# The joint input projection in token blocks of 128 columns instead of 256

## The chip, the cores and the metric

The kernel runs on one core of a Trainium2 chip. The metric is the device time of one execution in microseconds (us). The kernel before takes 576.53 us, the median of three runs from 575.89 to 577.66 us.

## What is computed

Two blocks follow each other. The first is an attention without softmax: a state per head decays with `w` and takes up `k` and `v` at each of 768 steps, for 4 batches of 8 heads of 48 elements. Its output becomes 3072 tokens of 384 elements, and these go through a feed-forward block with a gate.

```python
for t in range(S):
    cur = einsum('bhd,bhe->bhde', u[None] * k[:, :, t], v[:, :, t])
    y[:, :, t] = einsum('bhd,bhde->bhe', r[:, :, t], state + cur)
    state = w[:, :, t][..., None] * state + einsum('bhd,bhe->bhde', k[:, :, t], v[:, :, t])
x = y.transpose(0, 2, 1, 3).reshape(3072, 384)
h = x @ w_in                      # 384 x 2048
g = h * erf(softplus(h))
out = g @ w_out                   # 2048 x 384
```

All of it is fp32.

## The kernel before

The tokens go through in 12 units of 256 tokens (two batches of 128 tokens each, `UNIT = NJ * C` = 2 x 128). For each unit the attention makes `xT`, the unit's tokens with their 384 features on the partitions in three parts (`KT` = 3). The input projection makes the hidden values `h`, 2048 = 16 x 128 features by 256 tokens; softplus and erf on ScalarE and a multiply on VectorE make the gate; the output projection (`project_fast`, line 1245) uses a Strassen-like scheme with 192 columns per matmul. The engines' instructions are issued in an order written out by hand: strings such as `"J u v J J v J z z J"` name the next piece of work of each kind.

For most units the input projection is `hidden` (line 1123): three matmuls of 128 x 128 weights by 256 tokens accumulate one block of 128 features. For the last two units it is `hidden_of_two`. It treats the two units together as a product of 2 x 2 blocks and uses seven products with 128 x 128 weights, or sums of such weights, and tokens, or sums of tokens, instead of eight, and adds the products with the third part of the features. `join_weights` and `join_tokens` make the sums in advance. A `J` in the order is one step of it. Each step calls `add_up` once, which issues matmuls to one of three places in PSUM: `m0` (the tile `y`), `low` and `high` (two banks `pp`). Each place holds 2 x 256 values per partition, the two halves (`e`) in different PSUM banks. Behind `add_up` a copy on ScalarE (lines 1342, 1349, 1355) or a copy or add on VectorE (lines 1345, 1352, 1358, 1359, 1365) takes the sums out. `m0` gathers three products one after the other and is read out after each; the next pair of feature blocks starts it afresh. There are four pairs with seven steps each, and 88 matmuls in all.

The stage starts when the tokens of the last unit are there. While it runs, ScalarE and VectorE also make the gate of what is finished (`u`, `v`, `z` in the order, lines 1382, 1386 and 1390). Behind it come the output projections of the last units.

Two other places serve as measures below: line 641 (`level_products`) and line 748 (`state_part`) are small products of the attention, in which four tiles of TensorE's array are used in turn, each with weights of 32 to 64 columns; line 1033 transposes `k` with eight 128 x 128 matmuls against an identity.

Of the kernel before, what the change touches and what calls it, by code (L numbers as in the profile page):

```python
# [23 lines left out]
NJ = 2  # L24
# [38 lines left out]
def kernel(  # L63
# [14 lines left out]
    nc = tc.nc  # L78
    PSUM = bass.MemoryType.PSUM

    n_steps, _, _, JP, C = rkw.shape
# [52 lines left out]
    def products(shape, n=None):  # L134

        if n is None:
            n = turns["next"]
            turns["next"] = 1 - n
        names = "abc"[: len(shape) - 1]
        return banks[n][:].rearrange(  # L140
            f"p ({' '.join(names)}) -> p {' '.join(names)}", **dict(zip(names, shape[1:]))
        )
# [1138 lines left out]
    def third(g, kk):  # L1281

        return w_in_sb[:, g * FG : (g + 1) * FG, kk * P : (kk + 1) * P]
# [29 lines left out]
    def hidden_of_two():  # L1313

        one, two = n_steps - 2, n_steps - 1
        h11, h21 = (hid.tile([P, FG, UNIT], FP32, name="h")[:] for _ in range(NG))
        h12 = room[:, 2:4].rearrange("p i n -> p (i n)").rearrange("p (f t) -> p f t", t=UNIT)
        h22 = ins.tile([P, 2, JP, C], FP32, name="in")
        h22 = h22[:].rearrange("p x n t -> p (x n t)").rearrange("p (f t) -> p f t", t=UNIT)
        gated[one].extend((h11, h21))  # L1320
        gated[two].extend((h12, h22))
        m0 = y[:, :, 0].rearrange("p e j t -> p e (j t)")
        low, high = (products([P, NE, 2, UNIT], n)[:, :, 0] for n in range(2))

        s1, s2, s3, s4 = turns["joint weights"]
        x, z, t1, t2, t3, t4, less = turns["joint tokens"]
        a11, a12, up, _, a22, down = (third(g, kk) for g in range(NG) for kk in range(KT))

        def add_up(to, start, *factors):

            for k, (a, b) in enumerate(factors):
                for e in range(NE):
                    nc.tensor.matmul(  # L1333
                        to[:, e], lhsT=a[:, 2 * i + e], rhs=b,
                        start=start and not k, stop=True, skip_group_check=True,
                    )

        pairs = FG // 2
        for i in range(pairs):
            f = slice(2 * i, 2 * i + 2)  # L1340
            add_up(m0, True, (a11, x[0]))
            nc.scalar.copy(h11[:, f], m0)
            yield
            add_up(low, True, (a12, x[1]), (up, x[2]))
            nc.vector.tensor_add(h11[:, f], h11[:, f], low)
            chunks.append(h11[:, f])
            yield
            add_up(high, True, (s1, t1))
            nc.scalar.copy(h22[:, f], high)
            yield  # L1350
            add_up(m0, False, (s2, t2))
            nc.vector.tensor_copy(h12[:, f], m0)
            yield
            add_up(low, True, (a22, t4), (down, less))
            nc.scalar.copy(h21[:, f], low)
            yield
            add_up(m0, False, (s3, t3), (down, z[2]))
            nc.vector.tensor_add(h21[:, f], h21[:, f], m0)
            nc.vector.tensor_add(h22[:, f], h22[:, f], m0)
            chunks.append(h21[:, f])  # L1360
            if i < pairs - 2:
                chunks.append(h22[:, f])
            yield
            add_up(high, False, (s4, z[1]), (up, z[2]))
            nc.vector.tensor_add(h12[:, f], h12[:, f], high)
            if i < pairs - 2:
                chunks.append(h12[:, f])
            elif i == pairs - 1:
                chunks.extend(h[:, 2 * i - 2 : 2 * i + 2] for h in (h12, h22))
            yield  # L1370
# [136 lines left out]
    for kk in range(KT):  # L1507
        n = D // KT
        to, of = (x.rearrange("p (e m) -> p e m", e=NE) for x in (apart[:, kk], ident[:]))
# [190 lines left out]
```

## Time and profile before

| | |
|---|---|
| median of three runs | 576.53 us (575.89 to 577.66) |
| profiled execution, first to last instruction (the span) | 575.4 us |
| TensorE matmuls (PE) | busy 568.1 us, 99% of the span, 7336 instructions |
| TensorE weight loads (PEld) | busy 503.9 us, 88%, 7336 instructions |
| VectorE (DVE) | busy 442.7 us, 77% |
| ScalarE (ACT) | busy 358.0 us, 62% |
| GpSimd (POOL) | busy 244.7 us, 43% |
| granted TensorE clock | 1.000 over the whole span |

The profiled execution's own time is known as its span only: the page and the answer on cores both give 575.4 us from the first to the last instruction, 1.1 us below the median of the runs. The last matmul ends at 572.3 us and the last add on VectorE at 572.7 us; behind them comes only the last output's way out.

PE and PEld are two rows of one engine: weights for a following matmul are loaded while the present one runs. Recorded matmuls overlap, so the step from start to start is the time that one costs. Each fp32 matmul of the program appears as two passes in the trace, each a load and a matmul.

### The profile page before, as it was taken

To read this page: it belongs to the slowest core of one execution; us is meant where nothing else is said; L and a number is where in the kernel's file an instruction comes from. 1 tells how busy PE (TensorE), PEld (TensorE's weight loads), DVE (VectorE), ACT (ScalarE), POOL (GpSimd) and SP (SyncE) were. 2 spreads that over 40 slices of the span, in tenths; PEclk is the share of its full clock that TensorE was granted. 3 is DMA by queue.
4 is the path that set the end of the run, shared out by engine and by line. 5 is a ranking of instruction groups with operands and counts; after the bars stand their busy time and mean duration, and the time that the engine had idled before them with its cause. 6 is when DMAs were issued, how large, how long until landed. Compare 5 with 4: busy or idle time off the path is not lost.

```text
span 575.4 us, 16716 instructions
## 1 busy us (share of the span) xinstructions
PE 568.1 (99%) x7336; PEld 503.9 (88%) x7336; DVE 442.7 (77%) x475; ACT 358.0 (62%) x488; POOL 244.7 (43%) x265
## 2 busy tenths in 40 slices
PE   8999999999999999999999999999999999999997
PEld 6688777678998998998998998998898899988997
DVE  7785887999899998798699699599599527255640
ACT  3668777645458858748747756766766661388700
POOL 4567381632885883393384284185173000000000
PEclk9999999999999999999999999999999999999999
DMA  7595662350435325155145145234232201000000
GB/s 263 192 348 214 240 205 68 161 164 3 147 84 168 109 66 171 21 176 166 18 159 167 32 145 172 40 121 162 39 120 74 48 8 37 1 1 2 27 28 27
DMA packets 54081, 63.24 MB, mean 110 GB/s; under 512 B 35160, under 2 KB 40568, under 8 KB 52984
## 3 DMA queue, kind: packets, MB, share of 16 engines
q1 hardware_dynamic: 53624, 61.98, 34.0%
q8 instruction: 57, 0.93, 0.7%
q10 hardware_dynamic: 384, 0.20, 0.1%
q14 instruction: 16, 0.13, 0.1%
HBM read 52.39 MB, written 8.69 MB: 106 GB/s over the span
## 4 chain that ended last, share of the span: by engine, by line
PE 93%; DVE 4%; ACT 2%; issue 1%; POOL 0%; DVEq 0%; ACTq 0%; POOLq 0%
PE m L1245 34%; PE m L1123 33%; PE pp L641 5%; PE pp L1333 4%; PE m L1155 4%; PE y L1333 2%; PE y L673 2%; PE y L699 2%; PE pp L748 2%; PE m L951 1%; DVE in L334 1%; PE pp L960 1%; PE pp L1033 1%; DVE h L1088 1%; ACT rest L267 0%
## 5 line engine op out<-in xcount | busy, mean ns | idle before, releaser
L1123 PE MATMUL m<-xT,w_in_sb 128*128 128x256 f32 x960 | 215.0, 382 | 0.9 <-ACT h L1132 0.7
L1123 PEld LDWEIGHTS m<-xT,w_in_sb 128*128 128x128 f32 x960 | 179.8, 190 | 26.5 <-ACT h L1132 1.4
L334 DVE TENSOR_TENSOR in<-in,tot_sb 128x1024 f32<-128x1024 f32 (+1 forms) x55 | 80.1, 1457 | 12.7 <-PE pp L641 11.4
L1132 ACT COPY h<-m 128x512 f32<-128x512 f32 x80 | 46.1, 580 | 48.5 <-PE m L1123 48.4
L1245 PE MATMUL m<-mixed,h 128*128 128x192 f32 x320 | 56.7, 331 | 0.0
L1245 PE MATMUL m<-w_out_sb,h 128*128 128x192 f32 x320 | 56.2, 329 | 0.0
L1245 PEld LDWEIGHTS m<-mixed,h 128*128 128x128 f32 x320 | 51.8, 190 | 1.0
L1245 PE MATMUL m<-w_out_sb,room 128*128 128x192 f32 x304 | 52.5, 326 | 0.0
L1245 PEld LDWEIGHTS m<-w_out_sb,h 128*128 128x128 f32 x320 | 52.0, 190 | 0.5
L1245 PEld LDWEIGHTS m<-w_out_sb,room 128*128 128x128 f32 x304 | 49.9, 190 | 0.0
L1083 ACT ACT_TABLE_LOAD x30 | 38.5, 1283 | 10.7 <-DVE h L1088 8.5
L463 POOL TENSOR_TENSOR words<-words,own 128x384 f32<-128x384 f32 x21 | 30.1, 1432 | 22.8 <-DVE words L494 13.0
L504 POOL TENSOR_TENSOR words<-words 128x384 f32<-128x384 f32 x28 | 39.7, 1447 | 0.0
L1079 ACT ACT_TABLE_LOAD x30 | 38.5, 1283 | 1.8 <-issue 1.3
L641 PEld LDWEIGHTS pp<-in 48*48 48x48 f32 (+4 forms) x2368 | 30.1, 120 | 10.8 <-issue 3.5
L456 POOL TENSOR_TENSOR own<-rest 128x384 f32<-128x384 f32 x7 | 9.7, 1379 | 61.0 <-ACT o L1251 61.0
L641 PE MATMUL pp<-in 48*48 48x32 f32 (+4 forms) x2368 | 33.9, 206 | 0.2 <-DVE in L334 0.2
L504 POOL TENSOR_TENSOR rk<-words 128x384 f32<-128x384 f32 x28 | 33.4, 1220 | 0.0
L529 DVE TENSOR_REDUCE sums<-rk 128x16 f32<-128x768 f32 (+2 forms) x31 | 31.6, 1020 | 0.0
L408 POOL TENSOR_TENSOR tot_sb<-tot_sb 128x256 f32<-128x256 f32 (+4 forms) x50 | 28.8, 576 | 3.8
L1079 ACT ACTIVATE room<-h 128x1024 f32<-128x1024 f32 x28 | 29.6, 1057 | 0.3
L1245 PE MATMUL m<-mixed,room 128*128 128x192 f32 x160 | 27.7, 327 | 0.0
(206 smaller groups left out, 981.6 us busy)
## 6 DMA issues: line engine op xcount, KB each, us to landing
in<-in_rkw SPq DMA_DIRECT2D x8, 1024.0 KB, 5.2
words<-in_moe_w_in SPq DMA_DIRECT2D x16, 384.0 KB, 5.4
words<-in_moe_w_out SPq DMA_DIRECT2D x16, 384.0 KB, 5.2
words<-in_rk_rows SPq DMA_DIRECT2D x8, 768.0 KB, 6.1
w<-in_rkw SPq DMA_DIRECT2D x11, 512.0 KB
v<-in_v SPq DMA_DIRECT2D x12, 384.0 KB, 5.6
out<-o SPq DMA_DIRECT2D x23, 192.0 KB, 3.0
in<-in_rkw SPq DMA_DIRECT2D x7, 512.0 KB, 5.6
```

The lines of the kernel that those rows point to most:

```text
L334: nc.vector.tensor_mul(halves, halves, view(tots[level - 1], 0, [[1, n], [2, nb], [0, half]]))
L408: nc.gpsimd.tensor_mul(new, pair[:, :, 0], pair[:, :, 1])
L463: engine.tensor_mul(to, to, of[:, :, None, :].to_broadcast([P, NEAR // 2 // half, half, D]))
L504: engine.tensor_mul(to[:, i], r[:, half:], k[:, part * rows + i, None].to_broadcast([P, half, D]),)
L529: nc.vector.tensor_reduce(out=to, in_=of, axis=mybir.AxisListType.X, op=ALU.add)
L641: nc.tensor.matmul(to, lhsT=rk(1, n)[rows(e), s0 : s0 + m], rhs=right, start=True, stop=True,)
L1079: nc.scalar.activation(sp_room, chunks[0], AF.Softplus)
L1083: nc.scalar.activation(at, sp_room, AF.Erf)
L1123: nc.tensor.matmul(ps[:, ff, :], lhsT=w_in_sb[:, g * FG + f + ff, kk * P : (kk + 1) * P], rhs=xT[:, kk, :], start=kk == 0, stop=kk == KT - 1,)
L1132: nc.scalar.copy(h[:, f : f + FT, :], ps[:])
L1245: nc.tensor.matmul(to, lhsT=a[:, f], rhs=b[:, f], start=start and f == 0, stop=f == FG - 1, skip_group_check=True,)
L1333: nc.tensor.matmul(to[:, e], lhsT=a[:, 2 * i + e], rhs=b, start=start and not k, stop=True, skip_group_check=True,)
```

## The change

`add_up` issues, for each of its factors and halves, two matmuls of 128 token columns each instead of one of 256. Both use the same weights `a[:, 2 * i + e]`, and each brings its own load of them. The flag that starts a fresh sum in PSUM (`start`) is set on the first block of columns alone. Nothing else differs: the order of the work, the tiles, the instructions of the other engines and the engines that wait for each other are the same.

```diff
             for k, (a, b) in enumerate(factors):
                 for e in range(NE):
-                    nc.tensor.matmul(
-                        to[:, e], lhsT=a[:, 2 * i + e], rhs=b,
-                        start=start and not k, stop=True, skip_group_check=True,
-                    )
+                    for j in range(NJ):
+                        t = slice(j * C, (j + 1) * C)
+                        nc.tensor.matmul(
+                            to[:, e, t], lhsT=a[:, 2 * i + e], rhs=b[:, t],
+                            start=start and not (k or j), stop=True, skip_group_check=True,
+                        )
```

## The prediction

> **What bounds the kernel now.** I read the page first, for the engine that the end follows; then the windows of the stage that the change touches; then its groups and the chain of waits, for the time of one matmul instruction. From the page:
>
> ```profile
> PE 568.1 (99%) x7336; PEld 503.9 (88%) x7336; DVE 442.7 (77%) x475; ACT 358.0 (62%) x488; POOL 244.7 (43%) x265
> PE 93%; DVE 4%; ACT 2%; issue 1%; POOL 0%; DVEq 0%; ACTq 0%; POOLq 0%
> ```
>
> TensorE is busy 99% of the span and makes up 93% of the chain that ended last; its loader (PEld) is busy less. The stage of the change runs from the first L1333 matmul to the first L1245 matmul behind it (engines in the order PE, PEld, DVE, ACT, POOL, then granted clock, DMA share and GB/s):
>
> ```profile
> 492.57:530.56 37.99, 37.99 (x178) 33.23 (x177) 18.89 (x30) 27.92 (x42) 0.00 (x0) 1.00 0.00 1
> ```
>
> PE has no idle time in these 37.99 us, the clock is granted in full, DVE and ACT are busy 50% and 73%, and no DMA runs to speak of. So what the stage gains or loses on TensorE goes to the end one for one: behind it comes nothing but L1245 work, also back to back.
>
> ```profile
> L1333 PEld LDWEIGHTS pp<-xT,w_in_sb x48: 190/190/190, 493.2 to 530.1; 128*128 128x128 f32 x48
> L1333 PE MATMUL pp<-xT,w_in_sb x48: 379/379/380, 493.4 to 530.3; 128*128 128x256 f32 x48
> ...
> 493.60 2.59 PE pp L1333 x12
> ...
> 530.72 39.00 PE m L1245 x240
> ```
>
> The first two lines are of line 1333's own groups (ns min/median/max), the others of the chain of waits (start, us, what). The recorded 379 ns overlap: twelve passes take 2.59 us, 215.8 ns from start to start. The 192-column passes of L1245 take 39.00 / 240 = 162.5 ns, the 384-column ones of L1155 322.5 ns by their single starts. All three are N x 0.833 + 2.5 ns. The program has 88 matmuls in this stage and the trace 176 passes, so each fp32 matmul is two passes, each with a load of its own. 176 x 215.83 ns = 37.99 us, the stage.
>
> **What is removed, added, moved.** The same columns are moved, 176 x 256 = 352 x 128, in 352 passes, and 352 loads of 128 columns replace 176. No other engine's instruction changes. In the instruction order, waits stay on the first matmul of each product, ahead of the same work.
>
> The price is 352 x (new step) - 37.99 us. Two loops can set the step.
>
> The moving: by the law above a 128-column pass takes 106.7 + 2.5 = 109.2 ns. The trace has such passes, the transposes of L1033 (start, us, what):
>
> ```profile
> 50.44 1.09 PE L1033 MATMUL pp<-ident,in 128*128 128x128 f32 x8
> ```
>
> Taking off the last pass's own 0.272 us and the extra 0.057 us that the first one waits for its weights leaves 0.76 us for seven steps, 109 ns. 352 x 109.17 = 38.43 us: +0.44 us. This is the lower end, because no row has 128 columns moved in less; a gain is excluded, as the columns are the same and only the fixed 2.5 ns per pass doubles. The transposes don't show that the load keeps up: theirs is recorded with 141 ns, the stage's with 190 ns.
>
> The loading: now 216 ns lie between loads, and a load may take most of that unseen. At 128 columns the load (some 107 ns, below) is as long as the pass it must hide under. Rows in which the load sets the step are the level products of L641 and the state products of L748: four small tiles of the array work side by side there, and a tile loads as many columns as it moves, or more. Merged loads of L641 (start, us, what):
>
> ```profile
> 57.30 1.03 PEld L641 LDWEIGHTS pp<-rk 48*64 48x64 f32 x64
> 66.78 0.97 PEld L641 LDWEIGHTS pp<-in 48*60 48x60 f32 x64 [0.33 <-DVE y L276]
> 74.60 0.81 PEld L641 LDWEIGHTS pp<-in 48*48 48x48 f32 x64 [0.33 <-DVE in L334]
> ```
>
> 64 loads are 16 rounds of the four tiles. Without the last load (0.135, 0.132, 0.122 us) and the 0.020 us between the four, 15 rounds take 0.875, 0.818 and 0.668 us: about 58, 55 and 45 ns per round. The single starts give 58.3 ns for 64 loaded columns, 56.7 for 62, 55.0 for 60, 51.7 for 56, 45.0 for 48: exactly N x 0.833 + 5.0 ns, whether 32 or as many columns are moved. So a load overlaps the pass before it on the same tile, but a round of loads has 5 ns of its own where a pass has 2.5. The 64/64 row is this change in small: it takes 58.3 ns where the pass alone would allow 55.8 (as the 64-column passes of L673, with 48 loaded, do).
>
> For 128 columns this law gives 106.7 + 5.0 = 111.7 ns: 352 x 111.67 = 39.31 us, +1.32 us.
>
> The upper end is from the recorded lengths. In all those rounds the step is the load's recorded length less 77 ns (58.3 against 135, 45.0 against 122); 190 - 77 = 113 ns: 39.78 us, +1.79 us. The other way, where TensorE comes to whole-array products without a load in advance (the first L1123 pass behind L748), the next load starts 108 ns after the first one, and the second pass 320 ns after the first, which is 107 ns of load and 213 of moving: this points back to 109. I take 111.7, the value of the rows where load and pass are equally long and both repeat; both ends are kept for the range.
>
> What lies around: the consumers (ACT and DVE copies and adds of 512 columns) wait for a product's last pass, which now starts later but has half the columns (a recorded 272 instead of 379 ns), so they are released at the old time within 10 ns. The tightest turn is bank m0: the add of L1359 ends at 501.90 us and the next pair's first pass starts at 502.07, 0.17 us later. DVE starts its two adds when the last pass ends, and 8 (now 16) passes of `high` hide them: 9 x 215.8 - 379 = 1563 ns before, 17 x 111.7 - 272 = 1627 ns after, so the cover grows by 0.06 us; if it were gone, one add (0.69 us) in each of the three later pairs would cost 2.1 us. The 352 additional instructions on PE and on PEld cost nothing in fetching: elsewhere TensorE takes 352 pairs at 28.7 ns each (from 9 us on), and here one would come each 112 ns.
>
> Sum: 575.4 us span + 1.3 = 576.7 us. The median of the runs, 576.53 us, lies 1.1 us over the span; with the same distance the forecast is 576.53 + 1.32 = 577.85 us, say 577.9.
>
> **Rivals.**
>
> *Moving alone sets the step*, because the 5 ns of the load rounds belong to four tiles taking turns and not to one whole-array load. For: the 108 ns between the first two loads. Against: tile 0's own loop in L748 is 43 ns from load to pass and 2 ns from pass to the next load, with no time in which it visibly waits for the other tiles. 109.2 ns: 576.53 + 0.44 = 577.0 us.
>
> *A load has to be over, by its record, before its pass may start*; this is the one on the other side. The place is each of the 352 passes, the step 190 + 2 = 192 ns: 67.6 us, +29.6, 606.1 us. It decides as soon as less than 192 ns lie between passes. Against: L1245 has 190 ns loads at a step of 162.5 ns, so its passes start 28 ns before the recorded end of their load. What this can't exclude is some of it: a whole-array load that keeps up at a 162 ns step and not at 112. Each 5 ns over the forecast's step costs 1.76 us, so a step of 115 ns is +2.5 us, 579.0 us, and one of 125 ns +6.0 us.
>
> *Load and move in turn.* If the array didn't load while it moves, a step would be 107 + 109 = 216 ns: 352 x 216 = 76.0 us, +38, 614.6 us. Against: L1245 would then need 107 + 162 = 269 ns and shows 162.5. The Trainium skill's page "TensorE: Matmul & The Clock Gate" (Part 3, "The mechanism") has a rule that asks for this: weight loads overlap running matmuls only where the row group differs, and here every load and pass takes all rows. By that rule the trace disagrees, in L1245 (162.5 ns) as in L1333 (215.8 ns).
>
> *The change doesn't do what it says* (the second load of the same weights dropped) is out: the compiled order has four and eight matmuls of 128 columns for each two and four of 256, and a step can't go below the 109.2 ns of the moving in any case.
>
> **How the numbers follow.** Load rounds as in the small rows (111 to 113 ns): 0.65. Moving alone: 0.20. A whole-array load that falls somewhat short (113 to 190 ns): 0.10. A load over by its record: 0.03. In turn: 0.02. About 0.3% (1.7 us) is what a measurement of this kernel can tell from no change: the three runs before lie between 575.89 and 577.66. The forecast of +1.32 us is just inside that bound, and its upper end of +1.79 just outside, so I give a third of the first case (0.22) and nothing else of it to slower, with all of the last three (0.15): 0.37. Faster comes from scatter alone, 0.04, and 0.59 is left for the same. The range goes from the moving alone less the scatter of the runs below their median (577.0 - 0.6, rounded down: 576.3) to the upper end of the load with the scatter above it (576.5 + 1.8 + 1.1 = 579.4), and on to 580.5, which takes in a step of up to 116 ns (+2.8 us) with the same scatter.
>
> **What would show it.** Right: the stage lengthens from 38.0 to about 39.3 us, twelve old passes' work (24 new ones) take 2.68 us in the chain instead of 2.59, PEld is busy through the stage with no gap, recorded matmuls have 272 ns, and everything behind is shifted by the same 1.3 us. If passes start 109.2 ns apart, the first rival holds; above 115 ns a limit has appeared that no row shows here. An idle gap of PE ahead of `y` passes would mean that the m0 turn lost its cover. The prediction is wrong in kind if the stage keeps its length and the span changes elsewhere.

## The result and the profile after

The changed kernel takes 577.75 us, the median of 20 runs (576.81 to 580.40); the kernel before takes 576.64 us, the median of 20 runs beside it (575.50 to 577.96). The ratio is 1.0024, with a 95% interval from 1.0013 to 1.0034: +1.4 us, 0.7 to 2.0. It is not the quotient of the two medians, which lie 1.1 us apart.

The stage of the change in the trace after, from the first matmul of line 1335 to the first of L1245 behind it (columns as before):

```profile
491.34:530.64 39.30, 39.30 (x353) 39.30 (x353) 18.97 (x30) 28.19 (x42) 0.00 (x0) 1.00 0.01 2
```

The stage is 39.30 us long instead of 37.99. DVE and ACT have the work they had; PEld, busy 33.23 us before, is now busy in all of it. The groups of line 1335 (ns min/median/max) and the chain of waits (start, us, what):

```profile
L1335 PEld LDWEIGHTS pp<-xT,w_in_sb x96: 192/192/192, 492.1 to 530.4; 128*128 128x128 f32 x96
L1335 PE MATMUL pp<-xT,w_in_sb x96: 275/275/275, 492.2 to 530.5; 128*128 128x128 f32 x96
```

```profile
492.39 2.68 PE pp L1335 x24
...
530.80 39.00 PE m L1245 x240
```

24 passes take 2.68 us, 111.7 ns each; by their single starts every step in the stage is 111 or 112 ns but the first (110). The output projections behind it take 39.00 us as before.

The span of this execution is 575.5 us, only 0.1 us more than before. That isn't the change: TensorE reached the stage at 491.34 us instead of 492.57. Its first attention product began at 6.48 us instead of 7.09, and its first L1245 pass at 143.52 instead of 144.63, so 1.1 of the 1.2 us were gained in the first quarter, in code that is the same in both. In the experiments below that share this code, the stage begins between 491.79 and 492.93 us: the way to it varies by about as much as the change costs. The stage's own length and the medians of many runs carry the reading.

### The profile page after: what moved, and what is told of

Same layout as the page of the kernel before. It is cut to its first block, busy times and chain, and to the rows that moved or that the text cites. A ratio compares the mean times of both kernels' runs of the same rounds, so it can differ in the third digit from the quotient of the medians.

```text
span 575.5 us, 17068 instructions
## 1 busy us (share of the span) xinstructions
PE 568.4 (99%) x7512; PEld 509.7 (89%) x7512; DVE 439.7 (76%) x475; ACT 358.1 (62%) x488; POOL 245.9 (43%) x265
## 4 chain that ended last, share of the span: by engine, by line
PE 84%; DVE 7%; issue 3%; POOL 2%; DMA 2%; ACT 1%; SPq 0%; DVEq 0%; POOLq 0%; ACTq 0%
PE m L1245 34%; PE m L1123 29%; PE pp L641 5%; PE pp L1335 4%; PE y L1335 2%; DVE in L334 2%; PE y L673 2%; PE m L1155 2%; PE y L699 2%; PE pp L748 1%; DMA words<-in_moe_w_in 1%; PE pp L960 1%; DMA u_sb<-in_u 1%; DVE own L651 1%; POOL w_out_sb L1186 1%
## 5 line engine op out<-in xcount | busy, mean ns | idle before, releaser
L334 DVE TENSOR_TENSOR in<-in,tot_sb 128x1024 f32<-128x1024 f32 (+1 forms) x55 | 78.7, 1431 | 12.1 <-PE pp L641 10.8
L1245 PE MATMUL m<-mixed,h 128*128 128x192 f32 x320 | 56.7, 331 | 0.0
L1245 PE MATMUL m<-w_out_sb,h 128*128 128x192 f32 x320 | 56.1, 329 | 0.0
L1245 PEld LDWEIGHTS m<-mixed,h 128*128 128x128 f32 x320 | 51.7, 190 | 0.9
L1245 PE MATMUL m<-w_out_sb,room 128*128 128x192 f32 x304 | 52.5, 326 | 0.0
L1245 PEld LDWEIGHTS m<-w_out_sb,h 128*128 128x128 f32 x320 | 52.0, 190 | 0.5
L1245 PEld LDWEIGHTS m<-w_out_sb,room 128*128 128x128 f32 x304 | 49.9, 190 | 0.0
L1245 PE MATMUL m<-mixed,room 128*128 128x192 f32 x160 | 27.7, 327 | 0.0
```

What stands on the lines that cost most here:

```text
L334: nc.vector.tensor_mul(halves, halves, view(tots[level - 1], 0, [[1, n], [2, nb], [0, half]]))
L1245: nc.tensor.matmul(to, lhsT=a[:, f], rhs=b[:, f], start=start and f == 0, stop=f == FG - 1, skip_group_check=True,)
```

## The experiments

All times before are medians of the runs of the kernel before on the same chip. The ratios, with their 95% intervals, are again not quotients of the medians; +41.4 and +10.7 us below are differences of medians. The question was which loop sets the 111.7 ns, and whether it would do so elsewhere.

**More passes, the same loads.** Blocks of 64 token columns:

```diff
-                    for j in range(NJ):
-                        t = slice(j * C, (j + 1) * C)
+                    for j in range(4):
+                        t = slice(j * 64, (j + 1) * 64)
```

> Token blocks of 64 columns: 704 passes in the stage. Theory (the load of 128 weight columns sets the step, 128 x 0.833 + 5.0 = 111.7 ns, whatever is moved): the step stays 111.7 ns, the stage takes 704 x 111.67 = 78.6 us, +40.6 us on before, about 617 us in all. Rival 1 (every pass in a dense stream costs its columns and 5 ns): 704 x 58.33 = 41.1 us, +3.1 us. Rival 2 (the moving alone, 2.5 ns per pass): 704 x 55.83 = 39.3 us, +1.3 us.

617.83 us against 576.47, ratio 1.0702 (1.0677 to 1.0727), +41.4 us. The stage, its groups and the chain:

```profile
492.59:571.15 78.56, 78.56 (x706) 78.56 (x705) 19.33 (x30) 31.23 (x44) 0.00 (x0) 1.00 0.01 1
```

```profile
L1335 PEld LDWEIGHTS pp<-xT,w_in_sb x192: 192/192/192, 494.3 to 571.0; 128*128 128x128 f32 x192
L1335 PE MATMUL pp<-xT,w_in_sb x192: 275/275/275, 494.3 to 571.0; 128*128 128x64 f32 x192
```

```profile
494.49 5.36 PE pp L1335 x48
```

78.56 us for 704 passes, 111.6 ns each, with half the columns in each. A pass of 64 columns is recorded with the same 275 ns as one of 128, and only the stage's first pass, whose weights were loaded in advance, with 219. The 56 ns between them are what the step exceeds the moving of 64 columns by (111.7 - 55.8), so I read them as the wait for the load, recorded inside the pass. Both rivals, 58.3 and 55.8 ns per step, are out.

**As many passes, unequal.** Blocks of 192 and 64:

```diff
-                        t = slice(j * C, (j + 1) * C)
+                        t = slice(j * 192, 192 + j * 64)
```

> Blocks of 192 and 64 columns instead of 128 and 128: as many passes, loads and columns. Theory (a step is the longer of the pass and of the load under it): 162.5 ns from a 192-column pass to the next, 111.7 ns from a 64-column pass, 176 x 274.2 = 48.3 us, +10.3 us on before, about 587 us. Rival 1 (5 ns for each pass): 176 x (165.0 + 58.3) = 39.3 us, +1.3 us, no different from 128 and 128. Rival 2 (moving alone): 38.4 us, +0.4 us.

587.16 us against 576.47, ratio 1.0183 (1.0152 to 1.0214), +10.7 us. The stage and the groups of one tile by shape (busy us, mean ns, idle before):

```profile
492.20:540.40 48.20, 48.20 (x354) 48.20 (x353) 19.52 (x30) 29.66 (x43) 0.00 (x0) 1.00 0.01 1
```

```profile
L1335 PE MATMUL pp<-xT,w_in_sb 128*128 128x192 f32 x48 | 13.1, 354 | 0.0
L1335 PE MATMUL pp<-xT,w_in_sb 128*128 128x64 f32 x48 | 7.9, 247 | 0.0
```

The same number of loads, passes and columns as in the change costs 8.9 us more in the stage (48.20 against 39.30), because a long pass can't hide the load that belongs under a short one. The means are those of two kinds of pass. In the single rows half of the 192-column passes last 326 ns and half 382, half of the 64-column ones 219 and half 275: the longer half are those that begin behind a 64-column pass and wait 56 ns for their weights. As the wait is recorded inside the pass, single starts don't show the steps of 162.5 and 111.7 ns that were expected but about 162.5, 55.8, 111.7 and 218 ns in turn; the four add up to the same 548 ns. The 48.20 us rule out a fixed price per pass.

**The load a little shorter.** The load takes 120 or 126 of the 128 weight columns, the pass still 128 tokens:

```diff
-                            to[:, e, t], lhsT=a[:, 2 * i + e], rhs=b[:, t],
+                            to[:120, e, t], lhsT=a[:, 2 * i + e, :120], rhs=b[:, t],
```

> Blocks of 128 tokens, but each load takes 120 of the 128 weight columns; the last 8 features of each block of the joint projection are left out. Theory: the load loop is 120 x 0.833 + 5.0 = 105.0 ns and falls below the moving, so the step is 109.2 ns, the stage 38.4 us, +0.44 us on before. Rival 1 (5 ns for each pass): 111.7 ns and 39.3 us as with 128 weight columns, +1.3 us.

> As with 120 weight columns, but 126; the last 2 features of each block of the joint projection are left out. Theory: the load loop is 126 x 0.833 + 5.0 = 110.0 ns, still above the moving's 109.2, so the step is 110.0 ns and the stage 352 x 110.0 = 38.7 us, +0.73 us on before. Rival: loads are slower as soon as a whole array of 128 columns isn't loaded, or the 2.5 ns come in one step when load and pass are about equal: 109.2 or 111.7 ns.

With 120 columns 577.55 us against 576.47, ratio 1.0011 (0.9995 to 1.0027); with 126 columns 577.85 against 576.76, ratio 1.0019 (1.0006 to 1.0033). By the times alone the two can't be told from each other, nor from the change. The chain of waits can tell them: first 120 columns, then 126, and last the whole stage with 120.

```profile
493.06 2.62 PE pp L1335 x24
```

```profile
493.98 2.64 PE pp L1335 x24
```

```profile
492.03:530.45 38.42, 38.42 (x353) 38.42 (x353) 18.92 (x30) 28.03 (x42) 0.00 (x0) 1.00 0.01 2
```

By the single starts the steps are 109 or 110 ns (mean 109.2) with 120 columns and 110 with 126. The stages are 38.43 and 38.72 us, as expected, against 39.30 with 128 (with 126 columns from 492.93 to 531.65 us). So the step follows the weight columns down to 110.0 ns and then stops at 109.2, where the moving takes over. PEld is busy without a gap here too (38.42 us of 38.42), although the load no longer sets the step. This also measures the moving of 128 columns with ordinary weights, which the trace before had only for transposes.

**The neighbours' weights.** The loops over blocks and halves swapped, so that neighbouring matmuls never share their weights:

```diff
-                for e in range(NE):
-                    for j in range(NJ):
-                        t = slice(j * C, (j + 1) * C)
+                for j in range(NJ):
+                    t = slice(j * C, (j + 1) * C)
+                    for e in range(NE):
```

> The two loops swapped: blocks of 128 tokens outside, the two halves of the features inside, so that no two neighbouring matmuls share their weights. Theory: every pass brings its own load, so sharing weights with a neighbour neither helps nor costs; the step stays 111.7 ns, the stage 39.3 us, +1.3 us on before. Rival: the load of the same weights for a second time is what takes the 2.5 ns (or is cheaper than another load), and the step differs from 111.7 ns.

578.19 us against 576.76, ratio 1.0028 (1.0011 to 1.0044), the same as the change within the intervals. The stage is 39.30 us again, and its steps have the same counts of 111 and 112 ns. A load costs the same whether or not the matmul before it had the same weights. The two passes of one matmul stay neighbours in both orders, so nothing is shown for those.

**The same cut where the other engines work too.** In addition, the ordinary input projection of the other ten units is cut into blocks of 128 tokens (`start` is then set on the first matmul of each tile only; these lines are not shown):

```diff
+                        for j in range(NJ):
+                            t = slice(j * C, (j + 1) * C)
...
-                                ps[:, ff, :],
+                                ps[:, ff, t],
...
-                                rhs=xT[:, kk, :],
+                                rhs=xT[:, kk, t],
```

> The same change also in the ordinary input projection of the other ten units (L1123, 960 passes become 1920), where VectorE, ScalarE, GpSimd and DMA work beside it. Theory: 1920 x 111.67 - 960 x 215.83 = +7.2 us there and +1.3 us in the joint stage, +8.5 us on before, about 585 us. Rival 2 (moving alone): +2.4 and +0.4 us, +2.8 us. If other engines' reads and transfers slow the loads, more than 8.5 us and steps over 111.7 ns.

586.49 us against 576.47, ratio 1.0157 (1.0130 to 1.0185): +9.1 us, 7.5 to 10.7; the medians lie 10.0 us apart. One unit's projection in the chain of waits, first in the kernel before, then here, and a stretch of it here with all engines:

```profile
300.48 20.92 PE m L1123 x96
```

```profile
305.45 21.64 PE m L1125 x192
```

```profile
306.00:320.00 14.00, 14.00 (x128) 14.00 (x128) 13.96 (x12) 8.66 (x11) 6.87 (x13) 1.00 0.51 178
```

96 passes took 20.92 us, 192 take 21.64: +0.72 us for a unit, +7.2 for ten, as expected, and 8.5 us with the 1.3 of the joint stage, within the interval of the time. The steady steps are 111 and 112 ns here as well, with VectorE busy throughout, GpSimd half of the time and transfers at 178 GB/s. A slowdown of loads by other engines' work didn't show.

## Why the prediction was right

The forecast of 577.9 us for a measured 577.75 came out of the step that it took, 111.7 ns, and of the place where the step counts. That the median came within 0.2 us is partly luck, as the interval of the difference is 1.3 us wide; what bears the forecast out is the stage, 39.30 us for a forecast 39.31. Point by point:

- *What bounds the stage.* PE had no idle time before and has none after, and the L1245 work behind it takes 39.00 us in both, so the stage's gain or loss reached the end one for one: +1.32 us in the stage, +1.1 us between the medians.
- *The moving.* 109.2 ns was the lower end, from the transposes; the run with 120 weight columns shows 109.2.
- *The loading.* The law of the small tiles, 0.833 ns per column and 5.0 ns, was carried on from 64 columns on a quarter of the array to 128 on all of it. It gave a stage of 39.31 us, and 39.30 were measured; with 126 columns it gave 110.0 ns, and 110 were measured. The rival that the 5 ns belong to four tiles taking turns is out.
- *The signs named.* PEld without a gap was named as a sign that the forecast is right. It doesn't tell the load from the moving, as the run with 120 weight columns shows it as well. The step of 111.7 ns does.
- *The sum.* The 1.1 us between the span and the median before compare one execution with the median of others, and are no fixed distance: in the 20 runs after, each time lies 1.75 to 1.84 us over its own span. The forecast doesn't need it, as the 1.32 us are added to the median.
- *The upper end.* Recorded load length less 77 ns gave 113 ns and was wrong: these loads are recorded with 192 ns at a step of 111.7, a difference of 80. In these runs the recorded length of a load is no measure of its step.
- *A load over by its record, and load and move in turn.* A step of 111.7 ns is shorter than the 192 ns of the first of these rivals and the 216 ns of load and move together; the passes start 109 or 110 ns behind the start of their load, about 82 ns before its recorded end. The Trainium skill's page "TensorE: Matmul & The Clock Gate" (Part 3, "The mechanism") has a line that allows an overlap only where the row group differs, though the section also names a background weight buffer as a second case; by that line alone the trace disagrees here too, with every load on all rows.
- *The recorded passes.* 272 ns were forecast, 275 are recorded. The difference fits the wait for the load that the run with 64 columns shows: 2.5 ns is the gap between the two loops, 111.7 - 109.2. With 120 weight columns, where there is nothing to wait for, 272 or 273 are recorded.
- *The m0 turn.* The cover was to grow by 0.06 us. The add ends at 500.93 us and the next pair's first pass starts at 501.16, 0.23 us later; before it was 0.17.
- *The bound of 0.3%.* The prediction gave 0.59 to a change too small to tell at this bound. The ratio, 1.0024, lies inside it; its interval, 1.0013 to 1.0034, excludes no change and hardly reaches over 0.3%. The effect is real and small, and the trace shows it more sharply than the times.

What the runs leave open is the origin of the 5 ns: they show that it is there for 48 to 64 columns on small tiles and for 126 and 128 on the whole array, and not what makes it. One row of the kernel before doesn't fit the law at all, the loads of the transposes (ns min/median/max):

```profile
L1033 PEld LDWEIGHTS pp<-ident,in x32: 138/141/143, 50.4 to 171.7; 128*128 128x128 f32 x32
```

They load 128 columns into the whole array too, and by their single starts each but the first two of eight follows the one before in 109 to 111 ns, most in 109, in step with their passes; the law would make it 111.7. The prediction set them aside for their shorter record, 141 against 190 ns. They are also an exception to the two passes for each fp32 matmul, as eight transposes of the program are eight passes in the trace. Why their loads keep up with the moving isn't shown, so the law holds for ordinary matmuls only.

That it is the load which takes the 111.7 ns is in part argued. Every pass in these runs has its own load, and fewer weight columns also mean fewer columns of the array in the pass and fewer rows of its output, so a floor under the pass that grew with the weight columns would give the same steps. The transposes speak against such a floor: their passes have the same 128 x 128 shape and are recorded with the same 272 ns, and step at 109, and what differs in their records is the load.

## What to carry to other kernels

For fp32 matmuls that are no transposes and bring their own weights, take the longer of two loops as the step of a pass: columns moved x 0.833 + 2.5 ns (seen here from 64 to 384 columns), or weight columns x 0.833 + 5.0 ns (seen from 48 to 64 and at 126 and 128), at the granted clock of 1.00 that all these stages had. By an estimate from these two, 128 weight columns are hidden down to about 131 moved columns; at 128 the loss is 2.5 ns a pass, and below that each column saved in a pass saves nothing, so that blocks of 64 double the stage. Where a trace has no row for the size in question, rows in which the same loop binds at smaller sizes were a better measure here (111.7 ns) than recorded lengths (113 ns), which contain waits and overlaps.

## What the runs showed that was not expected

A matmul that waits for its weights isn't shown as idle: PE is 78.56 us busy in 78.56 with blocks of 64 columns, where half of the time is waiting. The sign of it is the length of the pass, 275 ns where 219 is the pass without a wait. PEld busy without a gap is no such sign: it is that with 120 weight columns too, where the passes have no wait.
